# Units of 1024 tokens in a two-layer feed-forward kernel: matmuls bank by bank, bank copies ahead of a cast, loads and sums of the first unit moved

## The chip, the cores and the metric

The program runs on one core of a Trainium2 chip. The metric is the time of one execution on the device in microseconds, and the median of several runs is compared. On this core TensorE (PE) multiplies, VectorE (DVE), ScalarE (ACT) and GpSimd (POOL) work on elements, and SyncE (SP) issues every DMA transfer from one queue, in program order.

## What is computed

The reference, cut to its core: attention in chunks of 64, then two feed-forward blocks with the same shape (4608 tokens, 512 features, 2048 hidden).

```python
def reference(q, k, v, w_in1, w_out1, w_in2, w_out2):
    x = chunked_attention(q, k, v)            # 8 x 8 x 576 x 64, softmax in chunks of 64
    x = x.transpose(0, 2, 1, 3).reshape(4608, 512)
    h = x @ w_in1
    x = (h * sigmoid(h)) @ w_out1
    h = x @ w_in2
    return (h * sigmoid(1.702 * h)) @ w_out2
```

Everything is float32. The kernel splits each operand of a product into a high part (a cast on ACT) and a low part (a subtraction on DVE) and forms three products of them (`TERMS`), so each float32 product costs three matmuls.

## The kernel before

The stretch that matters here is the second feed-forward block. Both of its products are done with seven products of quarter matrices instead of eight (the scheme of Strassen in Winograd's form): operands A11, A12, A22 and the sums S1 to S4, each multiplied with a weight quarter or a combination of weights (B11, B21, B22, T1 to T4). The weights are prepared earlier in the kernel and lie in DRAM; a tile `t` is 1 MB of them, and every operand has two such tiles for the second product.

**First product.** `in_products` (L664) goes through five widths `k` of the tokens, with eight rounds `j` each; a round is `round_of`, and its slots `extra(0)` to `extra(6)` run what the table `at_` puts there. The results (after the activation) are stored to DRAM as rows `g` by SP. In the rounds of the last width the table holds the preparations for the second product: weight tiles from `W_ORDER` and the loads and sums of the first unit.

**Second product.** `out_products` (L1048) covers 4096 tokens in four units of 1024 tokens; the last 512 tokens follow in a loop of its own (L829). A unit has 28 steps: for each operand of `SEQ` = A11, S1, A22, S2, S3, A12, S4 four steps (pairs of row tiles, `pp`). `step_d` (L960) issues the 12 matmuls of a step: two PSUM banks, two row tiles `c`, three terms. A11, S2 and S3 accumulate in the same two banks ("a"): S3 goes on adding where S2 has ended, and in between `finish_d` (L990) must copy both banks to SBUF, because the sum up to S2 is needed by itself. These copies are `copy_d` (L982) on ACT.

The order of the work is the order in which the code issues it; each engine runs its own instructions in that order. In step `g` the loop of `out_products` issues: the loads and sums of the table `at_d`; then the operand of step `g + 3`, `high_d` (L942, ACT, one cast of 128 x 1024) and `low_d` (L947, DVE); then a store; then, at the first step of an operand, the finish of the operand before; then a transpose; then the 12 matmuls:

```python
            if s % PAIRS == 0:
                late = finish_d((g - 1) // STEPS, SEQ[(g - 1) % STEPS // PAIRS])
            turn_d()
            step_d(u, s)
```

The operand buffers (pool `x`) are four, so the cast for step `g + 3` also waits until the matmuls of step `g - 1` have been read out. The sums S1 to S4 are made by POOL (`sum_d`, L927, 128 x 256 per instruction, four instructions per step's operand): S1 = A21 + A22, S2 = S1 - A11 in the same tile `mix`, S3 = A11 - A21 in the tile `a`, S4 = A12 - S2. Rows of A21, A22 and A12 come by `stream` (L909) into three buffers `rows_s`; A21 for the sums comes by `load_a21` (L902) into two tiles `mix`. POOL, like the others, works in program order.

Of the kernel before, what the change touches and what calls it, by code (L numbers as in the profile page):

```python
# [28 lines left out]
NOP = 7  # L29
# [20 lines left out]
def chunk_attention_two_ffn(  # L50
# [17 lines left out]
    KF = DFF // P  # L68
# [604 lines left out]
    def in_products(last):  # L673
# [4 lines left out]
        per = KF // 2  # L678
        for q in range(NQ):
# [3 lines left out]
            def at_(i, fn, *args):  # L683
                table.setdefault(i, []).append((fn, args))
# [46 lines left out]
                    at_(5, high_a, k + 1, S3)  # L731
                    at_(6, low_a, k + 1, S3)
            else:
                for m, what in enumerate(W_ORDER[:NOP * KF // 8 - 3]):
                    if (4 * m + 3) // NOP + 1 == j:
                        at_(6, *what)
                if j == per - 3:
                    at_(6, load_a21, 0, 0)
                    at_(6, stream, 0, "a22", 0)
                if j == per - 2:  # L740
                    at_(0, stream, 0, "a22", 1)
                    at_(2, sum_d, 0, S1, 0)
                    at_(4, sum_d, 0, S1, 1)
                    at_(6, high_d, 0, A11, 0)
                    at_(6, low_d, 0, A11, 0)
                if j == per - 1:
                    at_(0, load_a21, 0, 1)
                    at_(0, stream, 0, "a22", 2)
                    at_(0, high_d, 0, A11, 1)
                    at_(1, low_d, 0, A11, 1)  # L750
                    at_(2, stream, 0, "a22", 3)
                    at_(2, high_d, 0, A11, 2)
                    at_(3, low_d, 0, A11, 2)
                    at_(4, sum_d, 0, S1, 2)
                    at_(4, high_d, 0, A11, 3)
                    at_(4, low_d, 0, A11, 3)
# [120 lines left out]
    W_ORDER = []  # L877
# [83 lines left out]
    def step_d(u, s):  # L961

        o, pp = SEQ[s // PAIRS], s % PAIRS
        if pp == 0 and o in OPENS:
            open_banks(u, BANK[o])
        x = op_t.pop((u, o, pp))
        for c in range(2):
            for i, bank in enumerate(bank_u[u, BANK[o]]):
                for a, e in TERMS:
                    begins = o in OPENS and pp == 0 and c == 0 and (a, e) == TERMS[0]  # L970
                    nc.tensor.matmul(  # L971
                        out=bank,
                        lhsT=of_t(1, 2 * pp + c, WITH[o], e)[:, i * P:(i + 1) * P],
                        rhs=x[:, a, c],
                        start=begins,
                        stop=pp == PAIRS - 1 and c == 1 and (a, e) == TERMS[-1],
                        skip_group_check=o not in OPENS,
                    )
# [67 lines left out]
    def out_products():  # L1046
# [3 lines left out]
        def at_d(g, fn, *args):  # L1050
            todo.setdefault(g, []).append((fn, args))

        for m, what in enumerate(W_ORDER[NOP * KF // 8 - 3:]):
            at_d(1 + 2 * m, *what)
        at_d(1, sum_d, 0, S1, 3)
        def at_each(u, name, steps):
# [29 lines left out]
        for g in range(1, STEPS * NU):  # L1086
            u, s = divmod(g, STEPS)
            for fn, args in todo.get(g, ()):
                fn(*args)
            u3, s3 = divmod(g + 3, STEPS)  # L1090
            if u3 < NU:
                o3 = SEQ[s3 // PAIRS]
                high_d(u3, o3, s3 % PAIRS)
                low_d(u3, o3, s3 % PAIRS)
                if o3 == A22:
                    rows_s.pop((u3, "a22o", s3 % PAIRS))
            store_d()
            if late is not None:
                late()
                late = None  # L1100
            if s % PAIRS == 0:
                late = finish_d((g - 1) // STEPS, SEQ[(g - 1) % STEPS // PAIRS])
            turn_d()
            step_d(u, s)

        finish_d(NU - 1, SEQ[-1])
        for q in range(NR):
# [380 lines left out]
```

## Time and profile before

| | us |
|---|---|
| median of 3 runs | 1579.92 |
| lowest and highest of them | 1578.79 and 1584.04 |
| the profiled execution: time | 1578.65 |
| its span (first to last instruction) | 1576.9 |
| TensorE busy | 1548.5 (98% of the span) |
| VectorE, ScalarE, GpSimd busy | 882.0, 731.0, 416.3 |
| matmuls of the units (L971) | 1344 |

The profiled execution lasts 1.75 us longer than its span, and 1.27 us less than the median of the runs. The share of an engine says how much of the span it was busy; what a wait costs is read from the timeline of the engine that waits, since other engines may wait for nothing that matters.

### The profile page before, as it was taken

Reading aid. Unit: us, or ns where it says so; the run is one execution under the profiler, and the core shown is the slowest. Engines: PE = TensorE matmul, PEld = TensorE weight load, DVE = VectorE, ACT = ScalarE, POOL = GpSimd, SP = SyncE. Lnnn points to the kernel's source line nnn. Section 1 sums busy time; section 2 is a strip of 40 time slices with the busy share of each in tenths; the row PEclk is TensorE's granted clock in tenths of the full one; section 3 lists DMA queues with packets and bytes.
Section 4 is the critical chain, followed back from the end, with each engine's and each line's share of the span. In section 5 each row is a group of like instructions: output and inputs, shape, how many; then the busy total and the mean of one; then the engine's idle time right before and its main releaser. Section 6 shows DMA issues by size and latency. Waiting matters only on the chain.

```text
span 1576.9 us, 24560 instructions
## 1 busy us (share of the span) xinstructions
PE 1548.5 (98%) x9226; PEld 1286.8 (82%) x9226; DVE 882.0 (56%) x1453; ACT 731.0 (46%) x1046; POOL 416.3 (26%) x403
## 2 busy tenths in 40 slices
PE   8999999999999999999999999999999899999998
PEld 6878887888888888888888888888988687878788
DVE  6987666567657756665422242423424465757574
ACT  6774443454544444444323454545544434343432
POOL 1000010000000000000020030301304969797974
PEclk9999999999999999999999999999999999999999
DMA  9763443453444445453256343333369784858552
GB/s 249 210 148 90 114 137 99 113 141 101 134 115 131 104 110 133 107 139 101 96 195 223 122 158 133 135 141 140 129 243 372 279 210 146 233 156 222 146 131 73
DMA packets 352952, 242.83 MB, mean 154 GB/s; under 512 B 261696, under 2 KB 284224, under 8 KB 348224
## 3 DMA queue, kind: packets, MB, share of 16 engines
q1 hardware_dynamic: 352832, 241.25, 51.9%
q8 instruction: 72, 1.18, 0.3%
q14 instruction: 48, 0.39, 0.1%
HBM read 155.19 MB, written 85.98 MB: 153 GB/s over the span
## 4 chain that ended last, share of the span: by engine, by line
PE 81%; DVE 6%; DMA 5%; POOL 3%; issue 2%; ACT 2%; SPq 1%; DVEq 0%; ACTq 0%; POOLq 0%
PE acc L459 20%; PE h L424 20%; PE acc L577 18%; PE acc L971 10%; PE h L971 3%; PE h L577 3%; POOL a L927 2%; DMA rows_s<-g 2%; PE ps_at L292 2%; PE acc L829 1%; DVE aT L383 1%; DMA w<-split_u 1%; DVE g L447 1%; PE h L829 1%; DMA raw_w<-in_moe_w_in_dram 1%
## 5 line engine op out<-in xcount | busy, mean ns | idle before, releaser
L424 PE MATMUL h<-x,w 128*128 128x512 f32 x1728 | 419.5, 392 | 0.0
L459 PE MATMUL acc<-g,w 128*128 128x512 f32 x1728 | 416.4, 390 | 1.4 <-DVE w L155 1.2
L459 PEld LDWEIGHTS acc<-g,w 128*128 128x128 f32 x1728 | 323.6, 188 | 69.4 <-DVE w L155 1.9
L424 PEld LDWEIGHTS h<-x,w 128*128 128x128 f32 x1728 | 321.7, 188 | 68.9 <-issue 0.5
L577 PE MATMUL acc<-operand,t 128*128 128x512 f32 (+1 forms) x1200 | 274.3, 385 | 0.0
L577 PEld LDWEIGHTS acc<-operand,t 128*128 128x128 f32 x1200 | 222.4, 188 | 44.6
L971 PE MATMUL acc<-op,t 128*128 128x512 f32 x960 | 224.7, 395 | 11.7 <-ACT o L982 11.7
L199 POOL TENSOR_TENSOR raw_u<-raw_u 128x256 f32<-128x256 f32 x64 | 52.7, 846 | 687.9 <-DVE raw_u L139 544.4
L971 PEld LDWEIGHTS acc<-op,t 128*128 128x128 f32 x960 | 183.0, 191 | 51.9 <-ACT o L982 13.4
L435 ACT ACTIVATE s<-h 128x512 f32<-128x512 f32 x144 | 86.1, 598 | 298.8 <-PE h L424 293.9
L447 DVE TENSOR_TENSOR g<-s,g 128x512 fp32r<-128x512 f32 x144 | 100.1, 698 | 210.1 <-ACT g L437 208.9
L595 DVE TENSOR_TENSOR s<-acc,u 128x512 f32<-128x512 f32 (+1 forms) x80 | 51.0, 637 | 162.7 <-PE acc L577 120.0
L383 DVE STREAM_TRANSPOSE aT<-e 32x128 f32<-32x128 f32 x448 | 135.5, 302 | 6.0
L590 ACT COPY u<-acc 128x512 f32<-128x512 f32 (+1 forms) x80 | 43.5, 544 | 128.8 <-PE acc L577 128.5
L927 POOL TENSOR_TENSOR mix<-mix,rows_s 128x256 f32<-128x256 f32 x64 | 69.3, 1118 | 115.9 <-DMA rows_s<-g 84.2
L437 ACT CAST g<-s 128x512 fp32r<-128x512 f32 x144 | 89.5, 621 | 4.6
L971 PE MATMUL h<-op,t 128*128 128x512 f32 x384 | 88.3, 389 | 0.0
L947 DVE TENSOR_TENSOR op<-mix,op 128x1024 fp32r<-128x1024 f32 x48 | 67.1, 1403 | 35.5 <-ACT op L942 35.0
L603 ACT ACTIVATE s<-s 128x512 f32<-128x512 f32 (+1 forms) x120 | 70.9, 591 | 30.9 <-DVE s L595 30.4
L971 PEld LDWEIGHTS h<-op,t 128*128 128x128 f32 x384 | 72.1, 188 | 14.9
L942 ACT CAST op<-mix 128x1024 fp32r<-128x1024 f32 x48 | 50.3, 1053 | 72.2 <-PE h L971 36.8
L947 DVE TENSOR_TENSOR op<-rows_s,op 128x1024 fp32r<-128x1024 f32 x32 | 46.7, 1458 | 55.1 <-ACT op L942 48.4
(125 smaller groups left out, 1658.3 us busy)
## 6 DMA issues: line engine op xcount, KB each, us to landing
g<-s SPq DMA_DIRECT2D x128, 256.0 KB, 2.0
rows_s<-g SPq DMA_DIRECT2D x128, 256.0 KB, 3.0
t<-w SPq DMA_DIRECT2D x28, 1024.0 KB, 5.3
w<-split_u SPq DMA_DIRECT2D x16, 1024.0 KB, 4.2
w<-split_u SPq DMA_DIRECT2D x16, 768.0 KB, 4.4
x<-o SPq DMA_DIRECT2D x36, 256.0 KB, 2.3
raw<-in_q_dram SPq DMA_DIRECT2D x256, 32.0 KB, 2.2
raw<-in_k_dram SPq DMA_DIRECT2D x256, 32.0 KB, 2.3
```

The costliest lines, as they stand in the source:

```text
L199: nc.gpsimd.tensor_tensor(out=high[:, t - T1], in0=one, in1=two, op=ALU.subtract)
L383: nc.vector.transpose(out=aT_t[t0][to:to + 32, j, u], in_=e[of:of + 32, c, r])
L424: nc.tensor.matmul(out=h[:, :n], lhsT=w[:, 0, a, c * P:(c + 1) * P], rhs=x[b][:, c, :n], start=(c == 0 and (a, b) == TERMS[0]), stop=(c == ...
L435: nc.scalar.activation(out=s[:, :n], in_=h[:, :n], func=ACTF.Silu)
L437: nc.scalar.copy(out=g[:, 0, :n], in_=s[:, :n])
L447: nc.vector.tensor_tensor(out=g[:, 1, :n], in0=s[:, :n], in1=g[:, 0, :n].bitcast(F32), op=ALU.subtract)
L459: nc.tensor.matmul(out=a[:, :n], lhsT=w[:, 1, wi, i * P:(i + 1) * P], rhs=g[:, gi, :n], start=first and (wi, gi) == TERMS[0], stop=last an ...
L577: nc.tensor.matmul(out=bank[:, :n], lhsT=of_t(0, j, WITH[o], a)[:, c * P:(c + 1) * P], rhs=x[:, b, c], start=start and (c, a, b) == terms[ ...
L603: nc.scalar.activation(out=s[:, :n], in_=src[:, :n], func=ACTF.Silu, scale=act_scale[1])
L927: nc.gpsimd.tensor_tensor(out=out_[:, c, h], in0=one[:, c, h], in1=two[:, c, h], op=op)
L947: nc.vector.tensor_tensor(out=t[:, 1], in0=source_d(u, o, pp), in1=t[:, 0].bitcast(F32), op=ALU.subtract)
L971: nc.tensor.matmul(out=bank, lhsT=of_t(1, 2 * pp + c, WITH[o], e)[:, i * P:(i + 1) * P], rhs=x[:, a, c], start=begins, stop=pp == PAIRS - ...
```

## The change

Three edits.

- In `step_d` the two loops change places: first all six matmuls of one bank, then all six of the other, instead of three by three in turn.
- The finish of S2 (two copies on ACT) is issued right after the matmuls of S2's last step, and no longer in the step after, where it stood behind the cast for step `g + 3`.
- In the last width of the first product the loads and the first two sums S1 of unit 0 come earlier (first `mix` tile and first rows from round 5 to round 1, the further rows from rounds 6 and 7 to rounds 2 and 5, two sums from round 6 to round 4), and only 8 instead of 11 entries of `W_ORDER` are loaded in these rounds. The other 8 are loaded in steps 1, 3, ... 15 of unit 0, where before 5 of them were loaded in steps 1, 3, ... 9 and 3 in rounds 6 and 7.

```diff
             else:
-                for m, what in enumerate(W_ORDER[:NOP * KF // 8 - 3]):
+                for m, what in enumerate(W_ORDER[:8]):
                     if (4 * m + 3) // NOP + 1 == j:
                         at_(6, *what)
-                if j == per - 3:
+                if j == 1:
                     at_(6, load_a21, 0, 0)
                     at_(6, stream, 0, "a22", 0)
+                if j == 2:
+                    at_(6, stream, 0, "a22", 1)
+                if j == 4:
+                    at_(2, sum_d, 0, S1, 0)
+                    at_(6, sum_d, 0, S1, 1)
+                if j == 5:
+                    at_(0, stream, 0, "a22", 2)
+                    at_(6, stream, 0, "a22", 3)
                 if j == per - 2:
-                    at_(0, stream, 0, "a22", 1)
-                    at_(2, sum_d, 0, S1, 0)
-                    at_(4, sum_d, 0, S1, 1)
                     at_(6, high_d, 0, A11, 0)
                     at_(6, low_d, 0, A11, 0)
                 if j == per - 1:
                     at_(0, load_a21, 0, 1)
-                    at_(0, stream, 0, "a22", 2)
                     at_(0, high_d, 0, A11, 1)
                     at_(1, low_d, 0, A11, 1)
-                    at_(2, stream, 0, "a22", 3)
...
-        for c in range(2):
-            for i, bank in enumerate(bank_u[u, BANK[o]]):
+        for i, bank in enumerate(bank_u[u, BANK[o]]):
+            for c in range(2):
                 for a, e in TERMS:
...
-        for m, what in enumerate(W_ORDER[NOP * KF // 8 - 3:]):
+        for m, what in enumerate(W_ORDER[8:]):
             at_d(1 + 2 * m, *what)
...
-            if s % PAIRS == 0:
+            if s % PAIRS == 0 and SEQ[(g - 1) % STEPS // PAIRS] != S2:
                 late = finish_d((g - 1) // STEPS, SEQ[(g - 1) % STEPS // PAIRS])
             turn_d()
             step_d(u, s)
+            if s % PAIRS == PAIRS - 1 and SEQ[s // PAIRS] == S2:
+                finish_d(u, S2)
```

How this moves instructions, at three places. The names in the rows are line, operation, output and input; numbers behind a name are those of the buffer.

ACT in unit 0, from the first cast of S3's operand to the first of A12's. Before:

```order
L942 CAST op_11481<-a11_10808 128x1024
L942 CAST op_11499<-a11_10808 128x1024
L942 CAST op_11521<-a11_10879 128x1024
L942 CAST op_11540<-a11_10879 128x1024
L982 ACTIVATE o_11543<-acc0_11170 128x512
L982 ACTIVATE o_11545<-acc2_11171 128x512
L942 CAST op_11564<-rows_s_11451 128x1024
```

Now:

```order
L945 CAST op_11479<-a11_10816 128x1024
L945 CAST op_11497<-a11_10816 128x1024
L945 CAST op_11521<-a11_10890 128x1024
L985 ACTIVATE o_11536<-acc0_11166 128x512
L985 ACTIVATE o_11538<-acc2_11167 128x512
L945 CAST op_11544<-a11_10890 128x1024
L945 CAST op_11564<-rows_s_11447 128x1024
```

The two copies of the banks stood behind all four casts of S3; now they stand behind three, and the fourth cast comes after them.

PE in unit 0, the last step of S2 and the first of S3 (the weights `t` change between them). Before:

```order
L971 MATMUL acc0_11170<-op_11458,t_11111 128x512 x3
L971 MATMUL acc2_11171<-op_11458,t_11111 128x512 x3
L971 MATMUL acc0_11170<-op_11458,t_11111 128x512 x3
L971 MATMUL acc2_11171<-op_11458,t_11111 128x512 x3
L971 MATMUL acc0_11170<-op_11481,t_11200 128x512 x3
L971 MATMUL acc2_11171<-op_11481,t_11200 128x512 x3
L971 MATMUL acc0_11170<-op_11481,t_11200 128x512 x3
L971 MATMUL acc2_11171<-op_11481,t_11200 128x512 x3
```

Now:

```order
L974 MATMUL acc0_11166<-op_11432,t_11252 128x512 x6
L974 MATMUL acc2_11167<-op_11432,t_11252 128x512 x6
L974 MATMUL acc0_11166<-op_11454,t_11252 128x512 x6
L974 MATMUL acc2_11167<-op_11454,t_11252 128x512 x6
L974 MATMUL acc0_11166<-op_11479,t_11297 128x512 x6
L974 MATMUL acc2_11167<-op_11479,t_11297 128x512 x6
```

Of the rows now, the third and fourth are S2's last step and the last two S3's first. The first bank's last use in S2 lies six matmuls ahead of the step's end, and its first use in S3 follows right at the start of the next step.

SP around the second `mix` tile (round 7 of the last width). Before:

```order
L232 DMA t<-w_1_245 128x2048 x2
L902 DMA mix<-g_1_8_124 128x512
L902 DMA mix<-g_1_10_126 128x512
L902 DMA mix<-g_1_12_128 128x512
L902 DMA mix<-g_1_14_130 128x512
L909 DMA rows_s<-g_1_9_125 128x512
L909 DMA rows_s<-g_1_11_127 128x512
L909 DMA rows_s<-g_1_13_129 128x512
L909 DMA rows_s<-g_1_15_131 128x512
L605 DMA g_7_13_225<-s 128x512
```

Now:

```order
L605 DMA g_7_14_226<-s 128x512
L605 DMA g_8_12_240<-s 128x512
L905 DMA mix<-g_1_8_124 128x512
L905 DMA mix<-g_1_10_126 128x512
L905 DMA mix<-g_1_12_128 128x512
L905 DMA mix<-g_1_14_130 128x512
L605 DMA g_7_13_225<-s 128x512
```

The two weight tiles ahead of the `mix` tile and the four row loads behind it are gone from this place: the rows stand two rounds earlier, the tiles in the steps of unit 0.

## Rows read from the trace of the kernel before

**Rows 1.** Waits of PE from 850 us on: total us, times, longest us.

```profile
PE acc L971 <- ACT o L982: 11.7, 4, 6.1
```

**Rows 2.** Timeline of PE: start us, length us, operation, count [idle before <- releaser].

```profile
1231.21 11.04 PE L971 MATMUL h<-op,t 128*128 128x512 f32 x48
1242.09 11.04 PE L971 MATMUL acc<-op,t 128*128 128x512 f32 x48
1259.21 13.87 PE L971 MATMUL acc<-op,t 128*128 128x512 f32 x48 [6.08 <-ACT o L982]
...
1327.32 11.04 PE L971 MATMUL acc<-op,t 128*128 128x512 f32 x48
1340.29 11.19 PE L971 MATMUL acc<-op,t 128*128 128x512 f32 x48 [1.93 <-ACT o L982]
...
1405.71 11.04 PE L971 MATMUL acc<-op,t 128*128 128x512 f32 x48
1418.43 11.19 PE L971 MATMUL acc<-op,t 128*128 128x512 f32 x48 [1.68 <-ACT o L982]
...
1483.86 11.04 PE L971 MATMUL acc<-op,t 128*128 128x512 f32 x48
1496.96 12.77 PE L971 MATMUL acc<-op,t 128*128 128x512 f32 x48 [2.06 <-ACT o L982]
```

**Rows 3.** Timeline of ACT in units 0 and 2, around the copies of L982.

```profile
1253.90 1.05 ACT L942 CAST op<-a 128x1024 fp32r<-128x1024 f32 x1 [2.71 <-POOL a L927]
1257.61 1.04 ACT L942 CAST op<-a 128x1024 fp32r<-128x1024 f32 x1 [2.67 <-POOL a L927]
1258.57 1.08 ACT L982 ACTIVATE o<-acc 128x512 f32<-128x512 f32 x2
...
1414.12 1.06 ACT L942 CAST op<-a 128x1024 fp32r<-128x1024 f32 x1 [1.67 <-PE acc L971]
1416.84 1.04 ACT L942 CAST op<-a 128x1024 fp32r<-128x1024 f32 x1 [1.66 <-PE acc L971]
1417.79 1.08 ACT L982 ACTIVATE o<-acc 128x512 f32<-128x512 f32 x2
```

**Rows 4.** Two windows: us, busy us (x count) of each engine, PEclk, DMA share, GB/s.

```profile
1259.20:1263.00 3.80, 3.79 (x9) 3.02 (x10) 0.83 (x1) 0.44 (x1) 3.80 (x5) 0.50 0.97 328
...
1496.90:1500.00 3.10, 3.04 (x7) 2.37 (x8) 0.89 (x1) 0.50 (x2) 3.10 (x4) 0.53 0.45 153
```

**Rows 5.** Chain of waits: start us, us, 36 matmuls of the first product in a row.

```profile
1142.94 8.16 PE acc L577 x36
```

**Rows 6.** Timeline of POOL in unit 0: its sums S1 (two rows), S2, S3.

```profile
1203.06 9.61 POOL L927 TENSOR_TENSOR mix<-mix,rows_s 128x256 f32<-128x256 f32 x8 [81.03 <-DMA rows_s<-g]
1215.87 7.58 POOL L927 TENSOR_TENSOR mix<-mix,rows_s 128x256 f32<-128x256 f32 x8 [3.21 <-DMA rows_s<-g]
1223.41 16.20 POOL L927 TENSOR_TENSOR mix<-mix,a 128x256 f32<-128x256 f32 x16
1239.57 18.01 POOL L927 TENSOR_TENSOR a<-a,rows_s 128x256 f32<-128x256 f32 x16
```

**Rows 7.** Timeline of SP: issues of the second mix tile, and of step 1's weight tile.

```profile
1204.26 2.51 SPq L902 DMA_DIRECT2D mix<-g  x4
...
1216.48 0.39 SPq L232 DMA_DIRECT2D t<-w  x1
```

**Rows 8.** Line L902 (mix loads): us from issue to landing.

```profile
DMA to landing us min/median/max: 2.8/3.9/8.9
```

**Rows 9.** Timeline of DVE: low part of S1's first operand in unit 0.

```profile
1214.75 1.23 DVE L947 TENSOR_TENSOR op<-mix,op 128x1024 fp32r<-128x1024 f32 x1 [1.69 <-ACT op L942]
```

**Rows 10.** Windows as in rows 4, ahead of unit 0 and within it.

```profile
1165.00:1175.00 10.00, 10.00 (x46) 8.29 (x45) 2.08 (x3) 4.43 (x8) 0.00 (x0) 1.00 0.93 334
...
1225.00:1235.00 10.00, 10.00 (x46) 8.29 (x45) 4.73 (x4) 3.67 (x5) 10.00 (x9) 1.00 1.04 411
```

**Rows 11.** Chain of waits: a weight tile and a pair of rows, issue to landing.

```profile
1203.59 8.78 DMA t<-w
...
1234.94 6.24 DMA rows_s<-g
```

## The prediction

> **What bounds the kernel now.** I read the list of TensorE's waits first, because TensorE is busy in 98% of the span. After 850 us it names one wait only: the matmuls of L971 wait four times for the copies of L982 on ScalarE, 11.7 us in all, 6.1 the longest [rows 1]. The timeline of TensorE shows where. Each of the four units has the gap at the same place, between the last matmul of S2 and the first of S3 [rows 2]. Everywhere else in the units 48 matmuls (four steps) take 10.88 us from start to start (1231.21 to 1242.09), so a step is 2.72 us and a matmul 0.2267 us.
>
> The timeline of ScalarE shows why. In the third unit S2 ends at 1405.71 + 10.88 = 1416.59. At 1416.84 ScalarE begins a cast that isn't needed for another three steps, and only then makes the copies: the first starts at 1417.79 and TensorE goes on at 1418.43 [rows 2, 3]. That is a queue put in an awkward order. In the first unit the same cast also waits for GpSimd: it starts at 1257.61, 4.64 us after S2's end (1242.09 + 10.88 = 1252.97), because GpSimd's last sum S3 is late, and the copies behind it start at 1258.57 [rows 3, 6].
>
> A gap has a second price. After the first and the fourth the granted clock is 0.50 and 0.53, the lower level of 1.2 GHz [rows 4], and the 48 matmuls of S3 take 13.87 and 12.77 us long instead of 11.04. After the second and third they take 11.19 [rows 2].
>
> **The price of the four gaps.** The time lost is the start of S3 less the start of S2 less 10.88, plus S3's length less 11.04 [rows 2]:
>
> - unit 0: 1259.21 - 1242.09 - 10.88 = 6.24, and 13.87 - 11.04 = 2.83
> - unit 1: 1340.29 - 1327.32 - 10.88 = 2.09, and 0.15
> - unit 2: 1418.43 - 1405.71 - 10.88 = 1.84, and 0.15
> - unit 3: 1496.96 - 1483.86 - 10.88 = 2.22, and 12.77 - 11.04 = 1.73
>
> The gaps make 12.39 us and what follows them 4.86, together **17.25 us**.
>
> **The matmuls bank by bank.** 1344 matmuls change their order; none is added. Six in a row into one bank instead of three could cost or give something, and no unit shows it; but the first product runs exactly so, six to a bank, and its 36 matmuls take 8.16 us, 0.2267 each [rows 5], the pitch of L971. Cost: 0. What it buys: S2's first bank is done six matmuls, 1.36 us, ahead of S2's end.
>
> **The copies ahead of the cast.** Two copies take 1.08 us, so one about 0.54 [rows 3]. ScalarE's row before them is now the third cast of S3. In the third unit it starts at 1414.12, released by TensorE, and ends at 1415.18 [rows 3]; the first bank is ready at 1416.59 - 1.36 = 1415.23. The copy would run there, at once, and end near 1415.8, 0.8 us before S3's first matmul wants the bank. The second copy can start at S2's end and be done 0.6 us later; its bank is wanted 1.36 us after S2's end. So neither copy holds TensorE up, and the gap closes altogether. Units 1 and 3 have the same pattern. What is now queued behind the copies is the fourth cast: it starts some 0.6 us after S2's end, takes 1.05 and its low part on VectorE about as much again [rows 3, 9], and its matmuls come three steps, 8.16 us, after S2's end. Some 5 us are left. The next cast is held by its buffer for 2.72 us anyway, so nothing backs up. Gain of units 1 to 3: 2.24 + 1.99 + 3.95 = 8.18 us.
>
> **The first unit.** Here the copies wait behind the third cast, which GpSimd held up until 1253.90 [rows 3]. To be out of the way it should start when its buffer comes free, at S2's last step: 1252.97 - 2.72 = 1250.25. GpSimd must thus be 3.65 us earlier (2.9 are enough, since the copy has 0.8 us to spare). Its work in unit 0 is one chain from 1215.87 on, without a pause: half of S1, 7.58 us, S2 16.20, S3 18.01 [rows 6]. The chain starts late because it waits for rows (3.21 us), behind the first half of S1, which ends at 1203.06 + 9.61 = 1212.67.
>
> After the change that first half runs two rounds earlier, where GpSimd is idle (81.03 us of waiting stand in its row), and the rows for the second half are loaded before round 6. What the second half still waits for is the second `mix` tile, issued over 1204.26 to 1206.77 as before [rows 7], no longer with rows behind and two weight tiles ahead. Landing takes 2.8, 3.9 or 8.9 us (least, median, most) [rows 8]. With the median it starts at 1210.7 and ends at 1218.3, 5.1 us earlier than 1223.41; with the least the gain is 6.2, with the most 0.2. S2 can't start before VectorE has read the first S1 operand, 1214.75 + 1.23 = 1215.98 [rows 9], which is no limit here. I take the median: 5.1 us against 3.65 needed, a margin of 1.5 us, and the whole 9.07 us of this unit come back. At the lower end 3.8 to 4.8 of them come back (the first rival).
>
> **Transfers.** 12 rows of 256 KB, 3.15 MB, move from rounds 5 to 7 into the four rounds from the end of round 1 to the end of round 5. A round is 42 matmuls, 9.52 us, so they come to 83 GB/s on top of the 334 GB/s seen there [rows 10]. That makes 417, hardly more than the 411 of a later window [rows 10]; and nothing that is moved there is wanted before round 7. So I cost it at 0. If all of it had to be paid, 3.15 MB at 411 GB/s are 7.7 us, an upper bound. The Trainium skill (DMA: Bandwidth & Descriptors, "Where 436 GB/s comes from") puts what one core draws from HBM at about 358 GB/s. By that only 24 GB/s would be free, the rows would crowd each other, the first half of S1 would not be done early, and the time would be that of the first rival, near 1567.5. The 411 GB/s of the row are above that figure, so I side with the row.
>
> The eight weight tiles go the other way. S2's first tile is issued where step 1's tile is now, at 1216.48 [rows 7]; at 8.78 us, the longest landing on the chain [rows 11], it is there by 1226, and wanted at 1242.09. The last one, in step 15, is wanted at step 26, 1242.09 + 14 x 2.72 = 1280.2. Hidden: 0, at most the second rival.
>
> **The end.** The last 512 tokens follow TensorE's own progress (their loads are queued behind stores of results), so what is gained before them stays gained.
>
> **Sum.** 1578.65 - 17.25 = 1561.4 us for the profiled execution. The median of the runs lies 1.27 us above it, so I forecast 1579.92 - 17.25 = **1562.7 us**.
>
> **Rivals.**
>
> 1. *GpSimd is still late in unit 0.* The third cast ends at 1254.95, a copy takes 0.54, TensorE goes on near 1255.5: a gap of 2.5 us instead of 6.24, and a slow clock after it of 1.73 to 2.83 us, as after 2.06 and 6.08 us of idling. Time: 1562.7 + 2.5 + 2.3 = 1567.5. For it: the transfers are full just there, 0.93 and 1.04 of the engines [rows 10]. Against it: two weight tiles and four rows less stand around the tile that counts.
> 2. *The moved weights come too late* (the other side). SP issues in order, and in steps 1 to 15 the tiles now stand between row loads that wait for buffers which GpSimd and VectorE free. Tile number n of the eight lands at 1216.5 + n x d. The last is wanted at 1280.2, so d up to 8.0 us costs nothing; at 10 us TensorE waits some 16 us and the gain is gone (1579); beyond 10.7 us it is slower than before by over 0.3%. If the tiles came strictly after one another, each with 8.78 us, and 3 us more for the rows between them, d would be 11.8 and the time 1562.7 + 30.7 = 1593. Against it: transfers overlap, since at 411 GB/s a tile of 1 MB takes 2.6 us [rows 10].
> 3. *The first copy is released only at the step's end.* Then bank by bank buys nothing; each gap shrinks to a copy, about 0.6 us, and 0.15 after it, in four units: 1562.7 + 3.0 = 1565.7. That is also the case in which the reordering doesn't do what it says. Against it: TensorE goes on 0.1 us after the first copy already now (1417.79 + 0.54, 1418.43), so banks are waited for one by one [rows 2, 3].
>
> **How the numbers follow.** Forecast 0.72; rival 1 0.14; rival 3 0.06; rival 2 0.05 for a loss that about eats the gain, 0.03 for one beyond. A measurement of this kernel can tell 0.3%, 4.7 us, from no change; so faster 0.92, same 0.05, slower 0.03. The range goes from 1560, a little more under the forecast than the lowest run before lay under its median (1.1 us), to 1568, which takes in rivals 1 and 3; a little over 0.1 is left out.
>
> **What would show it.** Right: no wait of L971's matmuls for L982 (now L985) in the list, S3 starting 10.88 us after S2 in all four units and 11.04 us long, granted clock 1.00 there; GpSimd's first S1 sums before 1200 us and its S3 sums done before 1253; unit 0 from step 1 to its end without idling. Wrong: a wait for the low part of an operand or for a weight tile in TensorE's list, a start of GpSimd's second half of S1 after 1213, or matmuls of L974 more than 0.2267 us apart.

## The result and the profile after

| | before | after |
|---|---|---|
| median of the runs, us | 1579.36 (1576.2 to 1584.04, 6 runs) | 1565.38 (1563.46 to 1568.87, 6 runs) |
| profiled execution, us | 1578.65 | 1565.4 |
| its span, us | 1576.9 | 1563.6 |
| first matmul of the units, at us | 1206.70 | 1209.38 |
| from there to the first matmul of the last block, us | 324.64 | 308.69 |

The ratio is 0.9912, with a 95% interval from 0.9893 to 0.993. The change makes the kernel faster by some 14 us. The forecast was 1562.7 us with a range from 1560 to 1568, so the result is in the range and 2.7 us above the forecast.

The last row of the table is the measure for all that follows. If TensorE waited for nothing it would be 4 x 28 steps and one more step that is mixed with the first product: 113 x 2.72 = 307.36 us. Before, 17.28 us were lost; the prediction's four gaps and what follows them make 17.25. Now 1.33 us are lost.

The list of TensorE's waits in the changed kernel, from 850 us on (total us, times, longest us), answers to [rows 1]:

```profile
PE acc L974 <- ACT o L985: 0.8, 1, 0.8
```

The timeline of TensorE in the changed kernel, S2 and S3 of the four units, answers to [rows 2]:

```profile
1244.74 21.92 PE L974 MATMUL acc<-op,t 128*128 128x512 f32 x96
...
1320.90 21.92 PE L974 MATMUL acc<-op,t 128*128 128x512 f32 x96
...
1397.06 22.16 PE L974 MATMUL acc<-op,t 128*128 128x512 f32 x96
...
1473.46 11.04 PE L974 MATMUL acc<-op,t 128*128 128x512 f32 x48
1485.25 11.22 PE L974 MATMUL acc<-op,t 128*128 128x512 f32 x48 [0.75 <-ACT o L985]
```

In units 0 and 1 the 96 matmuls of S2 and S3 are now one row: no gap is left. In unit 2 the row is 0.24 us longer. In unit 3 the gap of 0.75 us is back as a row of its own. Windows of the same kernel over the starts of S3 (us, busy us of PE, PEld, DVE, ACT and POOL, PEclk, DMA share, GB/s) answer to [rows 4]; the granted clock is 1.00 where it was 0.50 and 0.53:

```profile
1255.00:1262.00 7.00, 7.00 (x33) 5.79 (x32) 3.90 (x3) 3.39 (x5) 7.00 (x6) 1.00 0.74 252
...
1484.00:1489.00 5.00, 4.25 (x19) 3.17 (x18) 1.85 (x2) 3.28 (x5) 5.00 (x7) 1.00 0.46 124
```

The timeline of ScalarE in the changed kernel, units 0 and 3, answers to [rows 3]:

```profile
1253.14 1.05 ACT L945 CAST op<-a 128x1024 fp32r<-128x1024 f32 x1 [1.66 <-PE acc L974]
1254.46 0.60 ACT L985 ACTIVATE o<-acc 128x512 f32<-128x512 f32 x1 [0.26 <-PE acc L974]
1255.82 0.60 ACT L985 ACTIVATE o<-acc 128x512 f32<-128x512 f32 x1 [0.76 <-PE acc L974]
1256.31 1.04 ACT L945 CAST op<-a 128x1024 fp32r<-128x1024 f32 x1
...
1483.65 1.05 ACT L945 CAST op<-a 128x1024 fp32r<-128x1024 f32 x1 [2.73 <-POOL a L930]
1484.61 1.08 ACT L985 ACTIVATE o<-acc 128x512 f32<-128x512 f32 x2
```

Unit 0 runs as the prediction drew it. S2 ends at 1244.74 + 10.88 = 1255.62; the first copy starts 1.16 us before that, is done at 1255.06, and S3 goes on at once. In unit 3 the third cast waits for GpSimd until 1483.65, the copies stand behind it, and S3 starts 0.91 us late. Before, the third cast waited for GpSimd in unit 0 alone (in units 1 and 3 the fourth did); now the last unit has the pattern of the first. The timeline of GpSimd in the changed kernel, which answers to [rows 6], shows why:

```profile
1208.39 7.58 POOL L930 TENSOR_TENSOR mix<-mix,rows_s 128x256 f32<-128x256 f32 x8 [26.88 <-DMA mix<-g]
1218.70 17.12 POOL L930 TENSOR_TENSOR mix<-mix,a 128x256 f32<-128x256 f32 x16 [2.73 <-DMA g<-s]
1237.12 17.09 POOL L930 TENSOR_TENSOR a<-a,rows_s 128x256 f32<-128x256 f32 x16 [1.30 <-DMA rows_s<-g]
...
1280.38 12.40 POOL L930 TENSOR_TENSOR mix<-mix,rows_s 128x256 f32<-128x256 f32 x12 [8.99 <-DMA mix<-g]
...
1358.39 17.70 POOL L930 TENSOR_TENSOR mix<-mix,rows_s 128x256 f32<-128x256 f32 x16 [8.70 <-DMA mix<-g]
...
1410.13 17.12 POOL L930 TENSOR_TENSOR mix<-rows_s,mix 128x256 f32<-128x256 f32 x16
1436.16 17.11 POOL L930 TENSOR_TENSOR mix<-mix,rows_s 128x256 f32<-128x256 f32 x16 [8.91 <-DVE turned L1030]
```

S3's sums of unit 0 are done at 1254.21, 44.83 us after the first matmul of the units; before it was 1257.58, or 50.88 us after. But GpSimd's S1 starts are 78.01 and 77.77 us apart, while TensorE's unit takes 28 x 2.72 = 76.16. Its four sums take 69.3 and 68.9 us; the rest is the 8.7 and 8.9 us of waiting ahead of the next S1. So GpSimd loses some 1.7 us on TensorE in each unit, and by unit 2 its lead is gone. What it waits for stands in SP's queue. The timeline of SP in the changed kernel at the end of unit 2:

```profile
1419.72 8.36 SPq L912 DMA_DIRECT2D rows_s<-g  x6
1428.17 4.91 SPq L1038 DMA_DIRECT2D out_dram<-turned  x8
1433.18 1.88 SPq L905 DMA_DIRECT2D mix<-g  x4
```

The mix load for the next S1 stands behind eight stores, and these behind row loads that take 8.36 us to issue, while GpSimd's S4 sums (1410.13 to 1427.25) still read the rows in whose buffers the new ones go. GpSimd holds up SP, and SP holds up GpSimd; an experiment below tests it.

That is new. SP's own waits (total us, times, longest us) in the kernel before, over 1412 to 1446 us:

```profile
SPq L909 <- DVE op L947: 9.3, 4, 5.2
...
SPq L909 <- POOL mix L927: 0.6, 1, 0.6
```

And in the changed kernel, over 1409 to 1436 us:

```profile
SPq L912 <- POOL mix L930: 8.3, 4, 2.9
...
SPq L912 <- DVE op L950: 1.4, 1, 1.4
```

Before, the row loads waited mostly for VectorE's reads of the rows (at 1422.59, 1425.31, 1428.03 and 1430.75 us, so 2.72 us apart, which is TensorE's step), and for GpSimd's S4 only once, 0.6 us. Now they wait for S4.

### The profile page after: what moved, and what is told of

It reads as the page before. It is cut to its first block, busy times and chain, and to the rows that moved or that the text cites. A ratio compares the mean times of both kernels' runs of the same rounds, so it can differ in the third digit from the quotient of the medians.

```text
span 1563.6 us, 24561 instructions
## 1 busy us (share of the span) xinstructions
PE 1544.6 (99%) x9226; PEld 1284.3 (82%) x9226; DVE 881.2 (56%) x1453; ACT 730.9 (47%) x1046; POOL 417.1 (27%) x403
## 4 chain that ended last, share of the span: by engine, by line
PE 86%; DVE 5%; DMA 2%; POOL 2%; ACT 2%; issue 2%; SPq 0%; DVEq 0%; ACTq 0%; POOLq 0%
PE acc L459 21%; PE h L424 21%; PE acc L577 19%; PE acc L974 12%; PE h L974 5%; PE h L577 3%; PE ps_at L292 2%; POOL mix L930 1%; PE acc L832 1%; DVE aT L383 1%; DMA w<-split_u 1%; PE h L832 1%; POOL a L930 1%; DVE g L447 1%; DMA v<-in_v_dram 0%
## 5 line engine op out<-in xcount | busy, mean ns | idle before, releaser
L974 PE MATMUL acc<-op,t 128*128 128x512 f32 x960 | 219.8, 389 | 0.8 <-ACT o L985 0.8
L930 POOL TENSOR_TENSOR mix<-mix,rows_s 128x256 f32<-128x256 f32 x64 | 64.8, 1049 | 105.1 <-DMA rows_s<-g 51.6
L950 DVE TENSOR_TENSOR op<-mix,op 128x1024 fp32r<-128x1024 f32 x48 | 65.9, 1374 | 38.6 <-ACT op L945 36.0
L517 POOL TENSOR_TENSOR s<-low 128x512 f32<-128x512 f32 (+1 forms) x10 | 12.6, 1278 | 235.9 <-DMA low<-x 146.8
```

The costliest lines, as they stand in the source:

```text
L930: nc.gpsimd.tensor_tensor(out=out_[:, c, h], in0=one[:, c, h], in1=two[:, c, h], op=op)
L950: nc.vector.tensor_tensor(out=t[:, 1], in0=source_d(u, o, pp), in1=t[:, 0].bitcast(F32), op=ALU.subtract)
L974: nc.tensor.matmul(out=bank, lhsT=of_t(1, 2 * pp + c, WITH[o], e)[:, i * P:(i + 1) * P], rhs=x[:, a, c], start=begins, stop=pp == PAIRS - ...
```

## The experiments

The table gives, for each profiled kernel, what each unit loses between the start of S2 and the end of S3 (start of A12 less start of S2 less 21.76 us; the row of the kernel before has the prediction's terms, which differ by up to 0.01 us of rounding), what is lost elsewhere in unit 0, the whole stretch, and the median with its ratio.

| kernel | unit 0 | 1 | 2 | 3 | elsewhere | stretch | median, ratio [95%] |
|---|---|---|---|---|---|---|---|
| before | 9.07 | 2.24 | 1.99 | 3.95 | 0.03 | 324.64 | 1579.36 |
| before, again | 9.04 | 2.00 | 3.96 | 4.56 | 0.59 | 327.51 | 1582.39 (one run) |
| banks only | 8.50 | 1.97 | 2.24 | 2.58 | 0.97 | 323.62 | 1579.7, 1.0 [0.999, 1.0011] |
| copies only | 4.55 | 0.34 | 0.84 | 1.41 | 1.41 | 315.91 | 1571.19, 0.9952 [0.9939, 0.9964] |
| loads only | 1.97 | 4.21 | 1.99 | 2.54 | 0 | 318.07 | 1573.05, 0.9967 [0.9954, 0.9979] |
| copies and loads | 0.34 | 0.32 | 0.30 | 1.57 | 0 | 309.89 | 1565.51, 0.9909 [0.9888, 0.9929] |
| tiles back | 0 | 0.95 | 3.98 | 0.23 | 0 | 312.51 | 1567.17, 0.9918 [0.99, 0.9936] |
| tiles later, rows not | 0.22 | 1.27 | 1.26 | 1.63 | 0 | 311.74 | 1567.77, 0.9924 [0.991, 0.9938] |
| whole change | 0 | 0 | 0.24 | 1.09 | 0 | 308.69 | 1565.38, 0.9912 [0.9893, 0.993] |
| whole, second time | 0 | 0.30 | 1.01 | 1.41 | 0 | 310.07 | 1564.89, 0.9914 [0.9901, 0.9928] |
| whole, third time | 0 | 0 | 0.52 | 2.34 | 0 | 310.22 | 1565.7, 0.9913 [0.9899, 0.9927] |
| whole, rows later | 0 | 0.02 | 0 | 0 | 0 | 307.38 | 1562.85, 0.9893 [0.9874, 0.9911] |
| rows later, again | 0 | 0 | 0 | 0 | 0 | 307.36 | 1562.32, 0.9891 [0.9877, 0.9905] |
| tiles back, rows later | 1.57 | 0 | 0 | 0 | 0 | 308.93 | 1563.32, 0.9895 [0.9879, 0.9911] |

**The three parts alone.** Each is a part of the diff shown above, put into the kernel before.

Copies only:

```diff
-            if s % PAIRS == 0:
+            if s % PAIRS == 0 and SEQ[(g - 1) % STEPS // PAIRS] != S2:
...
+            if s % PAIRS == PAIRS - 1 and SEQ[s // PAIRS] == S2:
+                finish_d(u, S2)
```

> The second edit alone: S2's copies are issued ahead of the next cast, matmuls bank after bank in threes as before, loads as before. The measure is the stretch of the units, from their first matmul to the first matmul of the last block: 324.6 us before (1206.70 to 1531.34), 308.7 after the change (1209.38 to 1518.07). Theory (the order on ScalarE makes the gap, the bank order adds little): units 1 to 3 have no gap or one of at most 0.2 us, because the second bank is wanted 0.68 us after S2's end and its copy is done after 0.6; unit 0 keeps about 2.5 us and a slow clock of 1.7 to 2.8 us behind it, because GpSimd still ends S3's third sum at 1253.9. Units 311.5 to 313, time 1567 to 1569. Rival (without the bank order the copies come too late): a gap of 0.6 us or more in every unit, units 314 to 315.

Banks only:

```diff
-        for c in range(2):
-            for i, bank in enumerate(bank_u[u, BANK[o]]):
+        for i, bank in enumerate(bank_u[u, BANK[o]]):
+            for c in range(2):
```

> The first edit alone: six matmuls to a bank in a row, copies and loads as before. Theory: the gaps stay as before (6.2, 2.1, 1.8, 2.2 us), since the copies still stand behind the cast; pitch 0.2267 us per matmul; units 324 to 325 us, time as before within 0.2%. Rival (an earlier end of the first bank is what helps): gaps shorter by 0.7 us or more each, units 321 or less. A rival on the other side (six in a row into one bank cost something): pitch above 0.23 us and units above 326.

Loads only: all hunks on `W_ORDER`, `load_a21`, `stream` and `sum_d`, and neither of the two above.

> The third edit alone: loads and sums of the first unit earlier, eight weight tiles later, the rest as before. Theory (unit 0's gap is the others' gap plus GpSimd's lateness): unit 0's gap falls from 6.2 to about 1.9 us, and what follows it from 2.8 to between 0.1 and 1.8; units 1 to 3 unchanged; units 316 to 318.5 us, time 1571 to 1573. Rival (the rows don't get there sooner, transfers being full): unit 0's gap above 5 us, units above 322.

The whole change, once more beside them:

> The changed kernel once more. Theory (the 2.7 to 3.0 us by which its units began later than before, first matmul of the first product at 867.0 against 864.0, are scatter of the stages ahead, which the change doesn't touch): the units take 308 to 310 us again, while the first matmul of the first product lies anywhere between 862 and 869, here and in the other three kernels, whether or not they hold an edit ahead of it. Rival (the change costs 3 us ahead of the units): 867 in the kernels with the third edit, 864 in those without.

The bank order alone is worth nothing, as expected. The copies alone take units 1 to 3 from 8.18 us to 2.59, but unit 0 only to 4.55 and 1.41 more; 315.91 us is longer than the theory and its rival said. GpSimd is late in unit 0, and its S1 starts are 77.6 us apart afterwards, more than TensorE's 76.16, so units 2 and 3 wait for it again. The timeline of TensorE with the copies alone, S2 and S3 of unit 0:

```profile
1244.22 11.04 PE L971 MATMUL acc<-op,t 128*128 128x512 f32 x48
1258.01 12.69 PE L971 MATMUL acc<-op,t 128*128 128x512 f32 x48 [2.74 <-ACT o L982]
```

That is the prediction's first rival (a gap of 2.5 us and a slow S3 after it), which the loads prevent. The loads alone do the opposite: unit 0 falls from 9.07 to 1.97, what the cast ahead of the copies costs in any unit, and units 1 to 3 keep their gaps. The parts nearly add up: 8.73 and 6.57 us saved alone, 14.4 to 16.0 by the whole change. Run once more, the whole change takes 310.07 us, and the first matmul of the first product is at 863.75 us, where the first profile of the change has 867.04 and the kernel before 864.00. So those 3 us are no cost of the change.

**The bank order beside the copies.** The whole change with the two loops in the old order:

```diff
-        for i, bank in enumerate(bank_u[u, BANK[o]]):
-            for c in range(2):
+        for c in range(2):
+            for i, bank in enumerate(bank_u[u, BANK[o]]):
```

> The change without its bank order (three matmuls by three in turn, as before): the early copies and the earlier rows stay. Measure: from the first matmul of the units to the first of the last block, 324.64 us before, 308.69 and 310.07 in two runs of the whole change, 307.36 if nothing waited. Theory: the bank order is worth only the earlier release of S2's first bank. Without it the first copy starts at S2's end, and S3 starts a copy and its wake-up late, 0.7 to 0.9 us, in the units where nothing else holds S3 up: units 0 and 1 for certain; in units 2 and 3 GpSimd's late sums hold the copies back anyway and little is added. So gaps of 0.7 to 0.9 us in units 0 and 1, and 310.0 to 312 us. Rival: the bank order is worth nothing beside the early copies, as it was worth nothing alone (1.000): no gap over 0.3 us in units 0 and 1, 308.5 to 310 us. Second rival: the late copies push the fourth cast of S3 so far that TensorE waits for it too, over 313 us.

The gaps are there in units 0, 1 and 2, but they are 0.30 to 0.34 us, not 0.7 to 0.9. The timeline of ScalarE in this kernel, unit 0, shows the error:

```profile
1252.60 1.05 ACT L945 CAST op<-a 128x1024 fp32r<-128x1024 f32 x1 [1.67 <-PE acc L974]
1254.60 1.28 ACT L985 ACTIVATE o<-acc 128x512 f32<-128x512 f32 x2 [0.94 <-PE acc L974]
1255.77 1.04 ACT L945 CAST op<-a 128x1024 fp32r<-128x1024 f32 x1
```

S2 ends at 1244.20 + 10.88 = 1255.08, and the first copy starts 0.48 us ahead of that. In the old order, too, the first bank is done before the step's end, by the three matmuls (0.68 us) of the other bank that come last. The new order adds another 0.68 us, of which some 0.34 are needed. Over four units that is 1.4 us at most, and less where GpSimd is late: the medians with and without it, 1564.89 to 1565.7 and 1565.51, don't tell them apart. The stretch of 309.89 us lies just under the theory's range and within the rival's.

**The weight tiles and the rows, each without the other.** The whole change with the tiles back where they stood:

```diff
-                for m, what in enumerate(W_ORDER[:8]):
+                for m, what in enumerate(W_ORDER[:NOP * KF // 8 - 3]):
...
-        for m, what in enumerate(W_ORDER[8:]):
+        for m, what in enumerate(W_ORDER[NOP * KF // 8 - 3:]):
```

> The change with the weight tiles back where they stood (three of them return to the rounds ahead of the units, five to six steps sooner); rows and sums of the first unit stay early. Measure: first matmul of the units to the first of the last block, 308.69 and 310.07 us with the whole change, 307.36 at best. Theory: the tiles have to move, because the transfers are full: 336 to 374 GB/s were moved there with the change, three tiles are 3.15 MB in some 40 us or 79 GB/s more, so 415 to 453, over the 411 to 414 of the fullest window. GpSimd then starts its second half of S1 up to 5 us later than the 1208.4 us of the changed kernel (two tiles of 2.6 us ahead of the mix tile), is late for S3 by 0 to 4 us, and unit 0 has a gap: 309.5 to 314 us, GpSimd's S2 sums later than 1220. Rival: only the earlier rows and sums matter, and the tiles could have stayed: unit 0 without a gap, 308.5 to 310.3 us as with the whole change.

The other half keeps the two `W_ORDER[8:]` lines, the copies and the bank order, and has rows and sums at their old rounds, as in the kernel before:

```diff
-                if j == 1:
+                if j == per - 3:
                     at_(6, load_a21, 0, 0)
                     at_(6, stream, 0, "a22", 0)
...
```

> The change with the first unit's rows and sums back at their old rounds: early copies, bank order and the later weight tiles stay. The other half of the run that put the tiles back. Measure: first matmul of the units to the first of the last block (307.36 us if nothing waits, 308.69 and 310.07 with the change), and GpSimd's start of the second half of S1 against the first matmul of the units: 9.2 us after it before, 10.9 after it with the early copies alone, 1.0 before it with the change. Theory: GpSimd's start is set by the rows, which the tiles only delay: taking three tiles away moves it by 1 to 4 us, not by 10; it comes 6 to 9 us after the first matmul, S3's sums are 2 to 4 us later than with the change (27.7 and 29.1 us after it), and unit 0 has a gap of 0.5 to 2.5 us that later units keep: 310 to 314 us. Rival: the tiles alone were the delay, GpSimd starts within 2 us of the changed kernel's, 308.5 to 310.3 us. Second rival: the rows need the tiles' place for nothing, start as with the early copies alone and 315 to 317 us.

Both halves are needed, but not where I had expected it: 312.51 and 311.74 us are within what the theories said, and yet either half alone gets unit 0 nearly right (0 and 0.22 us, where gaps were expected) and pays in units 1 to 3. With the tiles back the S2 sums start at 1219.17 us, not later than 1220. The kernel with the tiles back starts GpSimd's second half of S1 at 1211.62 us, 4.3 us after the first matmul of the units; the whole change starts it 1.0 us before that matmul. Windows of the kernel with the tiles back (columns as above), and the line of its mix loads over 1200 to 1212 us, show what delays it:

```profile
1165.00:1175.00 10.00, 10.00 (x46) 8.28 (x45) 2.08 (x3) 4.14 (x8) 1.98 (x3) 1.00 1.01 350
...
1205.00:1215.00 10.00, 10.00 (x45) 8.26 (x44) 5.57 (x6) 5.60 (x9) 3.38 (x5) 1.00 0.99 367
```

```profile
DMA to landing us min/median/max: 7.4/8.1/8.7
```

The transfers are full in both windows, two weight tiles are issued just ahead of the mix rows (at 1203.14 us), and the mix rows take 8.1 us to land. The same line in the changed kernel:

```profile
DMA to landing us min/median/max: 2.8/3.3/3.9
```

So moving the tiles isn't merely harmless: it makes the room for the second mix tile. In the kernel with the tiles later and the old rows, 80.87 us of waiting for rows still stand ahead of S1, then the 16 sums run in one go; S3's sums start 31.4 us after the first matmul of the units in place of 27.7 and 29.1. The timeline of its GpSimd:

```profile
1203.74 18.13 POOL L927 TENSOR_TENSOR mix<-mix,rows_s 128x256 f32<-128x256 f32 x16 [80.87 <-DMA rows_s<-g]
...
1238.90 17.10 POOL L927 TENSOR_TENSOR a<-a,rows_s 128x256 f32<-128x256 f32 x16
```

**GpSimd's round.** The whole change, with the third pair of rows for the next unit's S1 issued at step 24 in place of 21:

```diff
-                at_each(u + 1, "a22", (19 - STEPS, 20 - STEPS, 21 - STEPS, 26 - STEPS))
+                at_each(u + 1, "a22", (19 - STEPS, 20 - STEPS, 24 - STEPS, 26 - STEPS))
```

> The whole change, and the third pair of rows that is loaded for the next unit's S1 is issued three steps later (step 24 of the unit in place of 21). What it tests: with the change GpSimd's round of a unit takes 77.8 to 78.0 us where TensorE's takes 76.16, because GpSimd idles 8.6 to 9.0 us before each S1: it waits for the mix tile, whose load stands in SP's queue behind a row load that waits for GpSimd's own last sums. Theory: with the row load out of the way SP issues the mix load up to 4 us sooner, GpSimd's S1 starts are at most 76.5 us apart, the waits of S3 in units 2 and 3 (0.7 to 1.4 us) go, and first matmul to last block takes 307.4 to 308.5 us in place of 308.69 and 310.07; the time is 0.5 to 2 us under the whole change. Rival: the mix tile is held by something else (stores, or VectorE's reading of the old tile), S1 starts stay 77.5 us or more apart, 308.5 to 310.3 us. Second rival: the later rows themselves hold S1 up, over 310.3 us.

The theory holds, with two of its bounds a little tight: the S1 starts were to be at most 76.5 us apart, and the gain was larger than forecast. The timeline of SP in this kernel, the same place as above:

```profile
1415.87 5.55 SPq L912 DMA_DIRECT2D rows_s<-g  x4
1421.85 6.08 SPq L1038 DMA_DIRECT2D out_dram<-turned  x8
1428.03 1.86 SPq L905 DMA_DIRECT2D mix<-g  x4
```

The mix load comes 220.1 us after the first matmul of the units; with the change alone it was 223.8. GpSimd waits 6.51, 5.57 and 6.55 us ahead of S1, and its S1 starts (1278.25, 1354.95, 1430.94) are 76.70 and 75.99 us apart. The timeline of TensorE:

```profile
1243.25 21.92 PE L974 MATMUL acc<-op,t 128*128 128x512 f32 x96
...
1319.41 21.94 PE L974 MATMUL acc<-op,t 128*128 128x512 f32 x96
...
1395.59 21.92 PE L974 MATMUL acc<-op,t 128*128 128x512 f32 x96
...
1471.75 21.92 PE L974 MATMUL acc<-op,t 128*128 128x512 f32 x96
```

No gap is left in any unit. Once more, beside the whole change on one chip:

> The change with the third pair of rows three steps later, once more, timed beside the whole change on the same chip. Theory: 307.4 to 307.8 us from the first matmul of the units to the last block again, and a median 1 to 3 us under that of the whole change. Rival: the 307.38 us were luck, gaps of 0.5 us or more return in units 2 or 3, and the medians are within 1 us.

> The whole change a third time, beside the kernel with the later rows on the same chip. Expected: 308.5 to 310.3 us from the first matmul of the units to the last block, gaps of S3 in two or three of the units 1 to 3 where GpSimd is late, none in unit 0; first matmul of the units anywhere from 1206 to 1210 us.

The runs of the two don't overlap: 1561.31 to 1563.54 us with the rows later, 1565.35 to 1566.65 with the whole change alone. The kernel with the rows later is 3.4 us faster than the whole change, a little over the 1 to 3 us expected, and 17 us faster than the kernel before. Its stretch is 307.36 us again. The whole change, third time, lost 0.52 and 2.34 us in units 2 and 3; S2 and S3 of unit 3 in its timeline of TensorE:

```profile
1472.26 11.04 PE L974 MATMUL acc<-op,t 128*128 128x512 f32 x48
1485.30 11.22 PE L974 MATMUL acc<-op,t 128*128 128x512 f32 x48 [2.00 <-ACT o L985]
```

Last, the tiles back and the rows later together (the edits of both):

> The weight tiles back where they stood, as in the run before, and the third pair of rows three steps later, as in the run that reached 307.38 us. Putting the tiles back cost 5.15 us over 307.36, none of it in unit 0: GpSimd began its second half of S1 5.3 us later, still made S3 of unit 0 in time, but was late in units 1 and 2 (gaps of 0.65 and 2.08 us, the second with a slow S3). Theory: these gaps are GpSimd's lost lead, which it can't make up while its round takes 77.8 us against TensorE's 76.16; with SP out of its way a round takes 75.5 to 76.5 us when it is late, so the lateness doesn't grow: unit 1 has a gap of up to 0.9 us, units 2 and 3 none or less, 307.4 to 309 us. Rival: the tiles hurt by themselves (their transfers crowd rows in units 1 and 2 too), the gaps stay and it is 310 to 313 us.

GpSimd's second half of S1 came later still, at 1214.47, 7.1 us after the first matmul of the units, and the loss fell in unit 0 (1.57 us), not in unit 1. But from there the S1 starts are 76.07 and 76.85 us apart, and no later unit loses anything. So the 3.98 us of unit 2 with the tiles back were lost lead of GpSimd, not a second effect of the tiles.

**The kernel before, once more.**

> The kernel before once more, for a second profile. It is to show how far the parts of the saving scatter by themselves. Expected: first matmul of the units at 1206 to 1210 us (1206.09 to 1209.38 in the five profiles so far, so up to 3.3 us that no edit made); the gaps between S2 and S3 within 0.4 us of 6.24, 2.09, 1.84, 2.22; S3 after the first gap slow (granted clock near 0.5) again. If the clock falls after a 2.2 us gap by chance, S3 of the fourth unit is 11.2 us long here in place of 12.77, and first matmul to last block is 323.0 to 323.8 us; if by a rule that the length of the gap decides, it is 12.8 again, and 324.2 to 325.2 us.

The stretch is 327.51 us, outside of both expectations. The timeline of TensorE, units 2 and 3, and windows over the starts of S3 in these units:

```profile
1420.05 12.74 PE L971 MATMUL acc<-op,t 128*128 128x512 f32 x48 [2.11 <-ACT o L982]
...
1500.69 12.82 PE L971 MATMUL acc<-op,t 128*128 128x512 f32 x48 [2.62 <-ACT o L982]
```

```profile
1420.00:1423.00 3.00, 2.95 (x7) 2.38 (x8) 0.87 (x1) 0.48 (x1) 3.00 (x4) 0.50 0.94 329
1500.60:1503.70 3.10, 3.01 (x10) 2.39 (x11) 0.91 (x1) 0.53 (x2) 3.10 (x4) 0.72 0.42 152
```

Three of four gaps have a slow S3 here, two in the first profile [rows 2], and in the kernel with the banks alone only the first (13.28 us; the others 11.17 to 11.22). What follows a gap of 2 to 3 us thus varies between executions, and the gain read from one profile is uncertain by 2 to 3 us. The run doesn't settle chance against rule, since the gaps of units 2 and 3 (2.27 and 2.78 us) were longer than in the first profile, and by more than the 0.4 us expected. Two gaps of the same length that ended differently stand in the last section.

## Why the prediction was right, and where it was off

1. *Where the time is.* Right. Without gaps the stretch is 307.36 us, and 17.28 of the 324.64 us of before were the four gaps and what follows them.
2. *Unit 0, 9.07 us.* Right in all three profiles of the whole change. The copies wait for nothing, and S3 is 11.04 us long at full clock. The term's working was less good than its result: GpSimd's second half of S1 starts 1.0 us before the first matmul of the units, not 4.0 us after it. GpSimd then idles 2.73 us before S2, which starts at 1218.70, right after VectorE's read of the first operand (L950, from 1217.39, 1.22 us long); the row of this profile names a store as what ended the wait, that of the third profile names L950, after 2.09 us. The prediction had called that read no limit. Counted from the first matmul of the units, S3's sums end 6.05 us earlier, against 5.1 forecast and 3.65 needed.
3. *Units 1 to 3, 8.18 us.* This is the mis-sized term: the three profiles give back 6.85, 5.46 and 5.32 us. The step that failed is "Units 1 and 3 have the same pattern", with "nothing backs up" after it. The timeline of ScalarE in the kernel before, units 1 and 3, shows that they don't have the pattern of unit 2 [rows 3]:

```profile
1338.69 1.04 ACT L942 CAST op<-a 128x1024 fp32r<-128x1024 f32 x1 [1.92 <-POOL a L927]
...
1495.37 1.04 ACT L942 CAST op<-a 128x1024 fp32r<-128x1024 f32 x1 [2.05 <-POOL a L927]
```

   The fourth cast of S3 waited for GpSimd there, and for TensorE in unit 2. The prediction asked whether the copies delay a cast, and not whether GpSimd still delivers S3's sums in time once TensorE's unit shrinks to 76.16 us. In the three profiles GpSimd's S1 starts are 77.3 to 79.3 us apart. In the trace of before they are 78.7 us apart (1285.65, 1364.38 and 1443.10), beside 78.4 and 78.2 for TensorE with its gaps [rows 2]. That spacing by itself shows only that GpSimd kept TensorE's pace, not that its own round is too long. How little reserve it had shows in SP's waits above: one of the row loads ahead of its next mix tile waited for S4 already, 0.6 us, so S4 was done no earlier than VectorE's reads. The prediction looked at GpSimd in unit 0 alone. One of the signs that it had named failed with this term: the list still has a wait for the copies, 0.8 us in unit 3.
4. *Bank by bank at no cost.* Right: with the bank order alone the ratio is 1.0 [0.999, 1.0011]. What it buys was priced too high: the third rival took 0.75 us per unit without it, and 0.30 to 0.34 were measured.
5. *Transfers at no cost.* Right in the sum, wrong in its reason. I added 83 GB/s to 334 and held 417 to be hardly more than the 411 of [rows 10]. Windows of the changed kernel there, and around the second mix tile:

```profile
1165.00:1175.00 10.00, 10.00 (x46) 8.29 (x45) 2.52 (x4) 4.04 (x7) 2.82 (x4) 1.00 0.99 346
1175.00:1185.00 10.00, 10.00 (x46) 8.28 (x45) 2.08 (x3) 4.52 (x8) 2.83 (x4) 1.00 1.01 336
1185.00:1195.00 10.00, 10.00 (x46) 8.29 (x45) 2.07 (x3) 4.53 (x9) 0.00 (x0) 1.00 1.00 374
...
1205.00:1215.00 10.00, 10.00 (x46) 8.29 (x45) 6.33 (x6) 6.39 (x9) 6.61 (x7) 1.00 0.61 211
```

   Over 1165 to 1195 us the engines are full (share 0.99 to 1.01) at 336 to 374 GB/s: the 411 of another stretch was no measure for this one. It cost nothing because, as the prediction also says, nothing that is moved there is wanted before round 7; the first-half sums still ran at 1166.38 and 1178.68. The three tiles that left had stood in rounds 6 and 7, so they made no room here: with the tiles back, 1165 to 1175 us is as full (1.01 at 350 GB/s). They made room around the second mix tile, where the share is 0.61, and 0.99 with the tiles back. The Trainium skill (DMA: Bandwidth & Descriptors, "Where 436 GB/s comes from") gives about 358 GB/s for one core, against which I had sided with the row of 411. Over these 30 us the traces are nearer to that figure than to mine, but it is no ceiling in this case: full windows move 389 (1225 to 1235 us of the changed kernel) and 411 GB/s [rows 10]. What I derived from it, a late first half of S1, did not come.
6. *The moved tiles in time, and the tail.* Right: no wait for a weight tile stands in TensorE's list, and the stretch after the units takes 45.56 us before and 45.53 now.
7. *The sum.* Profile against profile the time falls by 1578.65 - 1565.4 = 13.25 us where 17.25 were forecast. Of the 4.0 that lack, 1.33 are point 3. The other 2.68 are a later start of the units, 1209.38 in place of 1206.70. It is there at the start of the first product already, ahead of every edit: 867.04 in place of 864.00, and in 14 profiles anywhere from 863.7 to 867.0. In three profiles of the same changed kernel the first matmul of the units is at 1206.09, 1207.90 and 1209.38. That is scatter; what makes it isn't settled.

That the result lies in the range owes something to luck: the range went up to 1568 for the sake of rivals 1 and 3, and what took 1.3 to 2.9 us of the gain was neither of them.

The forecast number was, in effect, that of the kernel with the rows later: 1562.3 and 1562.9 us measured, 1562.7 forecast for a change without any gap.

## What to carry to other kernels

When a gap of the busiest engine is closed, every other engine's round has to fit into the shorter one. Its start-to-start time of the same work in two rounds doesn't tell whether it will: an engine that follows the busiest one shows the old pace too (here 78.7 us beside 78.4 and 78.2). Look instead at what its waits hang on, at which engine is the last to release them before the change, and at how little separates it from the next; here hardly any reserve stood in the trace of before, and it cost 1.3 to 2.9 of the 17.25 us. An engine whose work takes 69 us of 76 can still be late because of a queue: look at what stands ahead of its loads in an in-order issuer, and move the one entry that waits for the late engine itself behind them. And where two moves fill and empty the same transfers, price them together.

## What the runs showed of the hardware

- The length of an idle spell alone didn't decide whether TensorE's clock fell. After gaps of up to 2.00 us the next 48 matmuls took 11.17 to 11.22 us. After 2.06, 2.08, 2.11, 2.62 and 2.74 us they took 12.69 to 12.82. But after 2.24 us (loads only, unit 3) they took 11.18, and after 2.29 us 11.17 in one kernel (banks only, unit 3) and 12.80 in another (loads only, unit 1). The granted clock in the windows of the kernel with the loads only, after its gaps of 2.29 and 2.24 us, is 0.64 (part of the window at the lower level) and 1.00:

```profile
1333.60:1336.70 3.10, 3.10 (x9) 2.48 (x10) 0.82 (x1) 0.44 (x1) 3.10 (x4) 0.64 0.95 326
1492.00:1495.10 3.10, 3.03 (x13) 2.53 (x14) 0.90 (x1) 0.51 (x2) 3.10 (x4) 1.00 0.36 135
```

- The rate at which the 16 DMA engines are full differs from stretch to stretch of one kernel: share 1.01 at 336 GB/s and 0.61 at 211 in the changed kernel, 1.04 at 411 in the kernel before [rows 10]. The mix rows of the second tile landed in 3.3 us (median) at the share of 0.61 and in 8.1 us at 0.99 (tiles back). Here the share told if there was room, and the GB/s of another stretch didn't.
